# Converted weights split into two whole rows, in a masked-attention and squared-Relu kernel on one core

## The chip, the cores and the metric

The kernel runs on one core of one Trainium2 chip. The time is the device time of one launch in microseconds (us). The engines are TensorE (PE), VectorE (DVE), ScalarE (ACT), GpSimd (POOL) and SyncE (SP), which here issues nearly all DMAs. A weight load of PE is an instruction of its own and runs beside matmuls; the profile calls it PEld.

## What is computed

Causal attention over a window of 128 keys, with a bias that falls linearly with distance, and then two matrix products with a squared Relu between them, all in float32:

```python
# q, k, v: (8, 8, 576, 64); w_in: (512, 2048); w_out: (2048, 512)
scores = (q @ k.T) / sqrt(64) - slope[h] * abs(i - j)     # where 0 <= i - j < 128, else -1e9
attn = softmax(scores)
x = (attn @ v) as (4608 tokens, 512)
h = maximum(x @ w_in, 0)
out = (h * h) @ w_out
```

## The kernel before

The 4608 tokens are cut into 9 chunks of 512 (c), the heads into 4 pairs (p), the 2048 inner columns into 16 blocks of 128 (f). Everything is kept transposed, with the 512 tokens of a chunk along the free axis.

Every float32 operand of a product is split into a high part that PE's fp32r takes exactly and a low part that holds the rest; three products (high x high, high x low, low x high) are summed. `gemm1(c, f)` (L170) makes 12 matmuls of 128 x 128 by 128 x 512 at L178 into the bank `g`, then Relu (L187, ACT), square (L190 on ACT in chunk 0, L193 on DVE later), the high part `hh` (L195, ACT) and the low part `hl` (L197, DVE). `gemm2(c, f)` (L199) makes 12 more at L208 into the four banks `acc`. After block 15 the four banks are copied to output tiles `o` (L220) and sent out (L221). Each matmul comes with its own weight load.

The weights come in as 64-bit floats in pairs of 32-bit words. `weights_load(f)` (L147) brings both matrices' block f as 8 KB a partition into slot f of an arena of 16 slots. `convert(f)` (L154) is five steps in place: two word shifts and a combination, then the high part `wh` (L164, ACT) over the high words and the low part `wl` (L166, DVE) over the low words. So high and low parts lie word by word next to each other, and a matmul's weights are every second word. Until the weights arrive, slots 11 to 15 of the arena serve as room for other things (score tiles `tw`, the bias table `wide`, zeros, the q, k and v of one pair).

The chunks run one after the other. `start` (L593) covers chunk 0: it builds a plan, a list of steps with engine, estimated time, predecessors and a due time, and issues them in the order in which a small list scheduler would run them; among steps that are ready at about the same time on an engine, the one with the earlier due time goes first. In it are: `heat` (L110), 16 pairs of matmuls on zeros of several kinds that fill PE at the beginning; the attention of chunk 0 in 8 segments (steps s, u, e, r, n, z, o, m, x, h, l); the attention of couples 4 to 8 (chunk 1 and the first pair of chunk 2; S scores, V values, `RING` their due times); the 16 conversions (`CONV` their due times, `HOLD` what they wait for); and the products of chunk 0, `gemm2` running two blocks behind.

After that (L706 on) the order on PE is the program's: `gemm1` of step n, `gemm2` of step n - 2, and in every eighth half step a visit, which finishes the values of one couple (`back`, matmuls at L329), loads q, k and v of the one after next, and scores the next (`front`, matmuls at L381, then soft-max on DVE, ACT and POOL). `FIRST` says at which half step the first visit stands. `turn` sends a 128 x 512 tile through DRAM to transpose it (L308 write, L313 read, both issued by SP) and masks the two copies on POOL (L317).

Of the kernel before, what the change touches and what calls it, by code (L numbers as in the profile page):

```python
# [9 lines left out]
F32 = mybir.dt.float32  # L10
F32R = mybir.dt.float32r
BF16 = mybir.dt.bfloat16
I32 = mybir.dt.int32
# [6 lines left out]
B, H, S, D = 8, 8, 576, 64  # L20
NP = H // 2
DM, DF = 512, 2048
NF = DF // 128
# [5 lines left out]
HOLD = lambda f: (('n', 3),) if f < 1 else (('n', 6),) if f < 2 else (('z', 7),)  # L29
# [1 line left out]
HAND = {"SP": 2.0, "PE": 0.25}  # L31
PORT = ('t', 'c', 'h1')
CONVERT = (('Activation', 1.2), ('DVE', 0.7), ('DVE', 1.2), ('Activation', 1.15), ('DVE', 1.2))
RING = lambda q: 50 + 20 * (q - 4)
CONV = lambda f: 28 + 5.5 * f
SOON = (("z", 7),)
FIRST = 35
SYNC = mybir.DependencyInfo(mybir.DependencyClass.Sync, mybir.DependencyReason.DATA)
CST = 256 + 128 * H
ENGINES = {e: getattr(mybir.EngineType, e) for e in ("PE", "DVE", "Activation", "Pool", "SP")}  # L40
# [6 lines left out]
class Kern:  # L47
    def __init__(self, ctx, tc, qkd, vd, w1d, w2d, cstd, outd):
        self.tc, self.nc = tc, tc.nc
        self.qkd, self.vd = qkd, vd  # L50
        self.w1d, self.w2d, self.cstd, self.outd = w1d, w2d, cstd, outd
        ep = lambda name, bufs, **kw: ctx.enter_context(tc.tile_pool(name=name, bufs=bufs, **kw))
        self.c = ep("const", 1)
        self.ld = ep("ld", 3)
        self.tp = ep("tp", 3)
        self.pp = ep("pp", 2)
        self.sm = ep("sm", 6)
        self.xu = ep("xu", 8)
        self.hp = ep("hp", 3)
        self.op = ep("op", 4)  # L60
        self.dr = ep("dr", 4, space=bass.MemoryType.DRAM)
        self.sc = ep("sc", 1, space=PSUM)
        self.at = ep("at", 1, space=PSUM)
        self.g1 = ep("g1", 1, space=PSUM)
        self.ac = ep("ac", 4, space=PSUM)
        self.cst = self.c.tile([128, CST], F32, name="cst")
        self.ident = self.cst[:, 0:128]
        self.mask = self.cst[:, 128:192].bitcast(I32)
        self.never = self.cst[:, 192:256]
        self.raw, self.w = [None] * NF, [None] * NF  # L70
        self.nc.alloc_sbuf_tensor("arena", [128, NF * 2048], F32)
        self.arena = self.nc.sbuf_base - NF * 8192
        self.x, self.qk, self.v, self.h, self.pairs = {}, {}, {}, {}, {}
        at = lambda slot, name, shape: self.nc.alloc_sbuf_tensor_at(name, shape, F32, offset=self.arena + slot * 4096).ap()
        self.wide = [at(2 * (NF - 3), "wide", [128, H, 256])[:, 2 * p : 2 * p + 2] for p in range(NP)]
        self.room_t = [at(2 * (NF - 5) + n, f"tw{n}", [128, 4, 256]) for n in range(4)]
        self.start_banks = [self.ac.tile([128, 512], F32, name="acc") for _ in range(4)]

    def nrel(self, h):
# [16 lines left out]


    def zeros(self):
        at = self.arena + (NF - 2) * 8192
        self.zb = self.nc.alloc_sbuf_tensor_at("zero", [128, 512], BF16, offset=at).ap()  # L100
        self.nc.vector.memset(self.zb, 0.0)
        zr = self.nc.alloc_sbuf_tensor_at("zeros", [128, 1024], F32R, offset=at + 1024).ap()
        self.nc.vector.memset(zr.bitcast(F32), 0.0)
        near = zr[:, 0:512]
        self.kinds = (
            (zr[:, 0:256:2], near), (zr[:, 0:128], near), (zr[:, 0:128], zr[:, 0:1024:2]), (zr[:, 0:64], near),
            (self.zb[:, 0:128], self.zb), (zr[:, 512:640], near),
        )

    def heat(self, n):  # L110
        g = self.g1.tile([128, 512], F32, name="g")
        w, x = self.kinds[4 if n < 4 else n % 6]
        for i in range(2):
            self.nc.tensor.matmul(g[0 : w.shape[1]], w, x, start=i == 0, stop=i == 1)  # L114

    def room(self, c, p, name, shape, offset):
        if (c, p) != (0, NP - 1):
            return self.ld.tile(shape, F32, name=name)  # L120
        at = self.arena + (NF - 1) * 8192 + offset
        return self.nc.alloc_sbuf_tensor_at(f"{name}_", shape, F32, offset=at).ap()

    def load_qk(self, c, p, sg):
# [21 lines left out]

    def weights_load(self, f):  # L147
        nc = self.nc
        at = lambda name, dt: nc.alloc_sbuf_tensor_at(f"{name}{f}", [128, 2, 512, 2], dt, offset=self.arena + f * 8192).ap()
        self.raw[f], self.w[f] = at("raw", I32), at("w", F32R)  # L150
        for i, d in enumerate((self.w1d, self.w2d.rearrange("(f p) d -> f p d", p=128))):
            nc.sync.dma_start(self.raw[f][:, i].rearrange("p d t -> p (d t)"), d[f].bitcast(I32))

    def convert(self, f):  # L154
        nc = self.nc
        lo, hi = self.raw[f][..., 0], self.raw[f][..., 1]
        flo, fhi, wl, wh = lo.bitcast(F32), hi.bitcast(F32), self.w[f][..., 0], self.w[f][..., 1]
        nc.scalar.activation(fhi, fhi, AF.Prelu, scale=2.0**-112, alpha=2.0**32)
        yield
        nc.vector.tensor_scalar(lo, lo, 29, None, op0=ALU.logical_shift_right)  # L160
        yield
        nc.vector.scalar_tensor_tensor(lo, hi, 3, lo, op0=ALU.logical_shift_left, op1=ALU.bitwise_or)
        yield
        nc.scalar.copy(wh, flo)  # L164
        yield
        nc.vector.tensor_tensor(wl, flo, wh.bitcast(F32), op=ALU.subtract)  # L166
# [3 lines left out]
    def gemm1(self, c, f):  # L170
        nc = self.nc
        xs = [self.x[c, p] for p in range(NP)]
        g = self.g1.tile([128, 512], F32, name="g")
        wh, wl = self.w[f][:, 0, :, 1], self.w[f][:, 0, :, 0]
        i = 0
        for cc in range(NCC):
            for w, part in ((wh, 0), (wh, 1), (wl, 0)):
                nc.tensor.matmul(  # L178
                    g, w[:, cc * 128 : cc * 128 + 128], xs[cc][:, part], start=i == 0, stop=i == 11
                )  # L180
                i += 1
        yield
        r = self.hp.tile([128, 512], F32, name="r", bufs=1)
        hh = self.hp.tile([128, 512], F32R, name="hh")
        hl = self.hp.tile([128, 512], F32R, name="hl")
        self.h[c, f] = hh, hl
        nc.scalar.activation(r, g, AF.Relu)  # L187
        if c == 0:
            yield
            nc.scalar.activation(r, r, AF.Square)  # L190
        else:
            yield
            nc.vector.tensor_tensor(r, r, r, op=ALU.mult)  # L193
        yield
        nc.scalar.copy(hh, r)  # L195
        yield
        nc.vector.tensor_tensor(hl, r, hh.bitcast(F32), op=ALU.subtract)  # L197

    def gemm2(self, c, f):  # L199
        nc = self.nc  # L200
        hh, hl = self.h.pop((c, f))
        if f == 0:
            self.acc = self.start_banks if c == 0 else [self.ac.tile([128, 512], F32, name="acc") for _ in range(4)]
        wh, wl = self.w[f][:, 1, :, 1], self.w[f][:, 1, :, 0]
        for m in range(4):
            ms = slice(m * 128, m * 128 + 128)
            for i, (w, h) in enumerate(((wh, hh), (wh, hl), (wl, hh))):
# [1 line left out]
                    self.acc[m], w[:, ms], h, start=(f == 0 and i == 0), stop=(f == NF - 1 and i == 2)  # L209
                )  # L210
            if f == NF - 1:
                o = self.op.tile([128, 512], F32, name="o")
                out = self.outd[m * 128 : m * 128 + 128, 512 * c : 512 * c + 512]
                if c == NCH - 1 and m == 3:
                    nc.scalar.copy(o[:, 0:256], self.acc[m][:, 0:256])
# [377 lines left out]
def start(K):  # L593
    P = Plan()
    for name, n in (("sc", 1), ("sa", 1), ("xa", 1), ("at", 1), ("zp", 1), ("tw", 4), ("t", 3), ("pp", 2), ("ld", 3), ("g", 1)):
        P.room(name, n)
    do = lambda fn, *a: lambda: fn(*a)
# [22 lines left out]

    P.add("zeros", "DVE", 0.4, (), -1, K.zeros)
    for n in range(HEAT):
        P.add(("heat", n), "PE", 0.9 if n < 4 else 0.45, ("zeros",) + ((("heat", n - 1),) if n else ()), 900 + n, do(K.heat, n), "g", "g")

    for k in range(8):
        G = Wide(K, k)
        c, p, sg = G.c, G.p, G.sg
        n = lambda s, *m: (s, k, *m)
# [6 lines left out]
            P.add(n("e", m), "Activation", 0.48 * w, (n("u", m),) + ((n("e", m - 1),) if m else ()), d + 0.5, do(G.exp, m))  # L635
        P.add(n("r"), "DVE", 0.4, (n("e", 3),), d + 1, G.sums)
        P.add(n("n"), "Pool", 2.05 * w, (n("r"),), d + 1, G.norm)
        P.add(n("z"), "PE", 0.9 * w, (n("n"),) + chain("z"), d - 1, G.turn, ("at", "zp", "pp"), "tw")
        P.add(n("o"), "Activation", 0.6, (n("z"),), d + 1, G.out, None, "at")
        P.add(n("m"), "DVE", 0.62 if w == 1 else 0.36, (n("z"),), d + 1, G.also, None, "zp")  # L640
        P.add(n("x"), "PE", 1.0, (n("m"), n("o"), ("v", c, p)) + chain("x"), d + 2, G.values, "xa", "pp")
        P.add(n("h"), "Activation", 0.4, (n("x"),), d + 2, G.high)
        P.add(n("l"), "DVE", 0.36, (n("h"),), d + 2, G.low, None, "xa")
        if sg == 1:
# [1 line left out]
    for q in range(4, 9):  # L646
# [7 lines left out]
        for s in (1, 0):  # L654
# [11 lines left out]
                continue  # L666
            step = do(next, G.squares(), None)
            P.add(n("square"), "DVE", 0.72, (n("n"),), d + 1, step, "pp", "t")
            P.add(n("write"), "SP", 1.6, (n("square"),), d + 1, step)
            P.add(n("read"), "SP", 2.2, (n("write"),), d + 1, step)  # L670
            P.add(n("before"), "Pool", 0.81, (n("read"),), d + 1, step)
            P.add(n("same"), "Pool", 0.81, (n("before"),), d + 1, step)
# [2 lines left out]
    for f in range(NF):  # L675
        d, last = CONV(f), ("w", f)
        g = K.convert(f)
        for i, (engine, us) in enumerate(CONVERT):
            P.add(("c", f, i), engine, us, (last,) + HOLD(f), d, lambda g=g: next(g, None))
            last = ("c", f, i)  # L680

    last = ["wide"] + [("l", k) for k in range(8)]
# [92 lines left out]
```

## Time and profile before

| | |
|---|---|
| time, median of 3 runs (lowest to highest) | 966.18 us (965.46 to 967.34) |
| the profiled execution, time / span | 967.88 us / 966.1 us |
| PE busy | 954.2 us, 99% of the span |
| DVE, ACT, POOL busy | 50%, 43%, 21% |
| granted PE clock, share of full | 0.999 |

The span is from the first to the last instruction; the profiled execution's own time holds some 2 us more. An engine's busy time counts its instructions and not its waiting. Matmuls overlap in the pipeline, so a group's busy time is less than its count times the mean of one. In the chain of waits each piece ends where the next begins, so there the length of 12 matmuls divided by 12 is the step from one to the next.

### The profile page before, as it was taken

To read this page: it belongs to the slowest core of one execution; us is meant where nothing else is said; L and a number is where in the kernel's file an instruction comes from. 1 tells how busy PE (TensorE), PEld (TensorE's weight loads), DVE (VectorE), ACT (ScalarE), POOL (GpSimd) and SP (SyncE) were. 2 spreads that over 40 slices of the span, in tenths; PEclk is the share of its full clock that TensorE was granted. 3 is DMA by queue.
4 is the path that set the end of the run, shared out by engine and by line. 5 is a ranking of instruction groups with operands and counts; after the bars stand their busy time and mean duration, and the time that the engine had idled before them with its cause. 6 is when DMAs were issued, how large, how long until landed. Compare 5 with 4: busy or idle time off the path is not lost.

```text
span 966.1 us, 17340 instructions
## 1 busy us (share of the span) xinstructions
PE 954.2 (99%) x6392; PEld 792.3 (82%) x6392; DVE 486.2 (50%) x1330; ACT 418.0 (43%) x1112; POOL 201.1 (21%) x252
## 2 busy tenths in 40 slices
PE   9899999999999999999999999999999999999998
PEld 5688887888888888888888888888888888888886
DVE  6898865444554444454545454444444454423222
ACT  7899754334433434334444444333433344322221
POOL 4122232222122222222121222122222222100000
PEclk9999999999999999999999999999999999999999
DMA  9983434222432223333422232233322231101001
GB/s 350 405 296 113 131 77 149 71 76 73 126 82 83 73 66 113 82 83 82 126 74 80 80 107 77 77 83 99 98 70 69 82 101 45 44 1 44 1 1 44
DMA packets 73028, 95.11 MB, mean 98 GB/s; under 512 B 8048, under 2 KB 42224, under 8 KB 72944
## 3 DMA queue, kind: packets, MB, share of 16 engines
q1 hardware_dynamic: 72512, 93.49, 32.0%
q8 instruction: 50, 0.82, 0.4%
q10 hardware_dynamic: 432, 0.52, 0.2%
q14 instruction: 34, 0.28, 0.1%
HBM read 67.76 MB, written 26.21 MB: 97 GB/s over the span
## 4 chain that ended last, share of the span: by engine, by line
PE 95%; DMA 2%; DVE 1%; ACT 1%; POOL 1%; issue 0%; SPq 0%; POOLq 0%; ACTq 0%
PE acc L208 41%; PE g L178 40%; PE at L329 6%; PE s L381 2%; PE g L381 2%; PE g L114 1%; DMA way<-pp 1%; DMA pp<-way 1%; PE acc L282 1%; PE s L496 0%; SPq L308 0%; PE at L528 0%; PE acc L496 0%; POOL pp L317 0%; PE at L381 0%
## 5 line engine op out<-in xcount | busy, mean ns | idle before, releaser
L178 PE MATMUL g<-xu,w 128*128 128x512 f32 x1728 | 426.9, 396 | 1.6 <-ACT r L187 1.6
L178 PEld LDWEIGHTS g<-xu,w 128*128 128x128 f32 x1728 | 337.2, 196 | 67.3 <-ACT r L187 3.4
L208 PE MATMUL acc<-hh,w 128*128 128x512 f32 x1152 | 388.0, 398 | 0.0
L208 PEld LDWEIGHTS acc<-hh,w 128*128 128x128 f32 x1152 | 225.3, 196 | 44.7 <-issue 0.5
L193 DVE TENSOR_TENSOR r<-r 128x512 f32<-128x512 f32 x128 | 92.5, 723 | 272.3 <-ACT r L187 272.2
L208 PE MATMUL acc<-hl,w 128*128 128x512 f32 x576 | 227.6, 395 | 0.0
L187 ACT ACTIVATE r<-g 128x512 f32<-128x512 f32 x144 | 85.5, 594 | 319.9 <-PE g L178 310.6
L317 POOL TENSOR_SCALAR_AFFINE_SELECT pp<-pp 128x512 f32<-128x512 f32 x128 | 103.7, 811 | 238.2 <-DMA way<-pp 129.7
L197 DVE TENSOR_TENSOR hl<-r,hh 128x512 fp32r<-128x512 f32 x144 | 107.8, 749 | 75.9 <-ACT hh L195 74.7
L195 ACT CAST hh<-r 128x512 fp32r<-128x512 f32 x144 | 89.2, 620 | 116.1 <-DVE r L193 115.5
L208 PEld LDWEIGHTS acc<-hl,w 128*128 128x128 f32 x576 | 112.8, 196 | 20.2
L253 POOL TENSOR_TENSOR t<-t,nm 128x512 f32<-128x512 f32 x64 | 73.3, 1147 | 252.7 <-DVE nm L250 220.5
L242 ACT ACTIVATE t<-t,nm 128x128 f32<-128x128 f32 x256 | 99.4, 390 | 37.1 <-DVE nm L235 37.1
L329 PEld LDWEIGHTS at<-pp,v 128*64 128x64 f32 x1024 | 55.2, 137 | 14.9 <-issue 10.4
L329 PE MATMUL at<-pp,v 128*64 128x128 f32 x1024 | 63.6, 276 | 2.7 <-POOL pp L317 2.6
L427 DVE COPY_PREDICATED t<-cst,s 64x256 f32<-64x256 int32 x100 | 44.3, 443 | 32.2 <-ACT t L415 18.5
L235 DVE CUSTOM_DVE_ANT_0 t<-t,cst 128x128 f32<-128x128 f32 x256 | 59.0, 294 | 0.9
L304 DVE STREAM_TRANSPOSE pp<-t 128x512 f32<-128x512 f32 x64 | 45.3, 708 | 23.9 <-POOL t L253 21.1
L242 ACT ACTIVATION_READ_ACCUMULATOR t<-t,nm 128x1 f32 x256 | 47.9, 187 | 0.0
L381 PE MATMUL s<-qk 64*64 64x64 f32 (+2 forms) x1168 | 47.5, 252 | 0.0
L381 PEld LDWEIGHTS s<-qk 64*64 64x64 f32 x1168 | 43.0, 134 | 0.0
L417 POOL MEMSET t<- 64x128 f32 (+1 forms) x44 | 10.0, 228 | 137.7 <-PE g L381 130.9
(65 smaller groups left out, 475.4 us busy)
## 6 DMA issues: line engine op xcount, KB each, us to landing
raw<-in_dram SPq DMA_DIRECT2D x32, 512.0 KB, 8.7
way<-pp SPq DMA_DIRECT2D x256, 64.0 KB, 1.8
pp<-way SPq DMA_DIRECT2D x64, 256.0 KB, 2.7
qk<-in_dram SPq DMA_DIRECT2D x32, 320.0 KB, 3.6
v<-in_dram SPq DMA_DIRECT2D x32, 320.0 KB, 2.9
qk<-in_dram SPq DMA_DIRECT2D x38, 256.0 KB, 4.2
out_dram<-o SPq DMA_DIRECT2D x35, 256.0 KB, 2.8
v<-in_dram SPq DMA_DIRECT2D x3, 256.0 KB, 4.6
```

The source lines that it names most:

```text
L178: nc.tensor.matmul(g, w[:, cc * 128 : cc * 128 + 128], xs[cc][:, part], start=i == 0, stop=i == 11)
L187: nc.scalar.activation(r, g, AF.Relu)
L193: nc.vector.tensor_tensor(r, r, r, op=ALU.mult)
L195: nc.scalar.copy(hh, r)
L197: nc.vector.tensor_tensor(hl, r, hh.bitcast(F32), op=ALU.subtract)
L208: nc.tensor.matmul(self.acc[m], w[:, ms], h, start=(f == 0 and i == 0), stop=(f == NF - 1 and i == 2))
L235: self.nc.vector.tensor_tensor_reduce(self.t[:, m], self.t[:, m], self.K.nrel(2 * self.p + m // 2), -0.125, BIG, ALU.add, ALU.min, self.nm ...
L242: self.nc.scalar.activation(self.t[:, m], self.t[:, m], AF.Exp, bias=nm[:, m : m + 1], scale=-1.0, accum_out=nm[:, 4 + m : 5 + m],)
L253: self.nc.gpsimd.tensor_tensor(self.t, self.t, self.nm[:, 8:12].unsqueeze(2).to_broadcast([128, 4, 128]), op=ALU.mult)
L317: nc.gpsimd.affine_select(to, self.own, pattern=[[-32 * sign, 4], [0, 4], [-sign, 32]], compare_op=op, fill=0.0, base=0, channel_multiplie ...
L329: self.nc.tensor.matmul(self.X[r, o : o + 128].rearrange("p (a c) -> p a c", a=4), v[:, 2 * sg + k, r], src[:, :, 2 * j + i], start=sg == ...
L381: mm = nc.tensor.matmul(to, qk[r, q0 : q0 + 64], qk[r, k0 : k0 + 64 * n], start=True, stop=True, skip_group_check=True,)
```

## The change

The arena gets a seventeenth slot. Raw words of block f go to slot f + 1, the converted weights of block f to slot f, as [low or high][matrix][512], so each part is one row of 512 words per matrix. The write of `wh` of block f overwrites raw words of block f - 1, so a predecessor is added: the last step of the conversion of block f - 1. The rooms that share the arena move up one slot. The pool of four output tiles goes, and four quarters of the spare slot take its place. The heats are all bf16. Visits come two half steps (one product pair) later. Some due times and one predecessor change, and with them the order in which steps are issued.

```diff
-RING = lambda q: 50 + 20 * (q - 4)
-CONV = lambda f: 28 + 5.5 * f
-SOON = (("z", 7),)
-FIRST = 35
+RING = lambda q: 50 + 18 * (q - 4)
+CONV = lambda f: 34 + 5.5 * f
+SOON = (("x", 7),)
+FIRST = 37
@@ Kern.__init__
-        self.op = ep("op", 4)
...
-        self.nc.alloc_sbuf_tensor("arena", [128, NF * 2048], F32)
+        self.nc.alloc_sbuf_tensor("arena", [128, (NF + 1) * 2048], F32)
...
+        o = at(2 * NF, "o", [128, 4, 512])
+        self.o = [o[:, m] for m in range(4)]
@@ heat
-        w, x = self.kinds[4 if n < 4 else n % 6]
         for i in range(2):
-            self.nc.tensor.matmul(g[0 : w.shape[1]], w, x, start=i == 0, stop=i == 1)
+            self.nc.tensor.matmul(g, self.zb[:, 0:128], self.zb, start=i == 0, stop=i == 1)
@@ weights_load
-        at = lambda name, dt: nc.alloc_sbuf_tensor_at(f"{name}{f}", [128, 2, 512, 2], dt, offset=self.arena + f * 8192).ap()
-        self.raw[f], self.w[f] = at("raw", I32), at("w", F32R)
+        at = lambda slot, name, shape, dt: nc.alloc_sbuf_tensor_at(f"{name}{f}", shape, dt, offset=self.arena + slot * 8192).ap()
+        self.raw[f] = at(f + 1, "raw", [128, 2, 512, 2], I32)
+        self.w[f] = at(f, "w", [128, 2, 2, 512], F32R)
@@ convert
-        flo, fhi, wl, wh = lo.bitcast(F32), hi.bitcast(F32), self.w[f][..., 0], self.w[f][..., 1]
+        flo, fhi, wl, wh = lo.bitcast(F32), hi.bitcast(F32), self.w[f][:, 0], self.w[f][:, 1]
@@ gemm1
-        wh, wl = self.w[f][:, 0, :, 1], self.w[f][:, 0, :, 0]
+        wh, wl = self.w[f][:, 1, 0], self.w[f][:, 0, 0]
@@ gemm2
-        wh, wl = self.w[f][:, 1, :, 1], self.w[f][:, 1, :, 0]
+        wh, wl = self.w[f][:, 1, 1], self.w[f][:, 0, 1]
...
-                o = self.op.tile([128, 512], F32, name="o")
+                o = self.o[m]
@@ start
-        P.add(n("z"), "PE", 0.9 * w, (n("n"),) + chain("z"), d - 1, G.turn, ("at", "zp", "pp"), "tw")
+        P.add(n("z"), "PE", 0.9 * w, (n("n"),) + chain("z"), d - 5.5, G.turn, ("at", "zp", "pp"), "tw")
...
-        P.add(n("x"), "PE", 1.0, (n("m"), n("o"), ("v", c, p)) + chain("x"), d + 2, G.values, "xa", "pp")
+        P.add(n("x"), "PE", 1.0, (n("m"), n("o"), ("v", c, p)) + chain("x"), d + 4, G.values, "xa", "pp")
...
-            P.add(n("write"), "SP", 1.6, (n("square"),), d + 1, step)
+            P.add(n("write"), "SP", 1.6, (n("square"),), d - 4, step)
...
-            P.add(("c", f, i), engine, us, (last,) + HOLD(f), d, lambda g=g: next(g, None))
+            free = (("c", f - 1, len(CONVERT) - 1),) if f and i == 3 else ()
+            P.add(("c", f, i), engine, us, (last,) + HOLD(f) + free, d, lambda g=g: next(g, None))
```

## Rows read from the trace of the kernel before

**Rows 1.** The page: busy time of PE, and the chain's shares by line.

```profile
PE 954.2 (99%) x6392; PEld 792.3 (82%) x6392; DVE 486.2 (50%) x1330; ACT 418.0 (43%) x1112; POOL 201.1 (21%) x252
...
PE acc L208 41%; PE g L178 40%; PE at L329 6%; PE s L381 2%; PE g L381 2%; PE g L114 1%; DMA way<-pp 1%; DMA pp<-way 1%; PE acc L282 1%; PE s L496 0%; SPq L308 0%; PE at L528 0%; PE acc L496 0%; POOL pp L317 0%; PE at L381 0%
```

**Rows 2.** The chain in order of time: start, length (us), what.

```profile
53.11 2.80 PE g L178 x12
...
214.68 2.76 PE g L178 x12
```

**Rows 3.** Groups by line and form: busy us, mean ns | idle before.

```profile
L178 PE MATMUL g<-xu,w 128*128 128x512 f32 x1728 | 426.9, 396 | 1.6 <-ACT r L187 1.6
...
L178 PEld LDWEIGHTS g<-xu,w 128*128 128x128 f32 x1728 | 337.2, 196 | 67.3 <-ACT r L187 3.4 <-issue 0.3
```

**Rows 4.** Timeline of PE where it waits: start, length (us), what [wait].

```profile
42.82 3.10 PE L178 MATMUL g<-xu,w 128*128 128x512 f32 x12 [1.59 <-ACT r L187]
...
137.46 2.33 PE L329 MATMUL at<-pp,v 128*64 128x128 f32 x32 [0.59 <-POOL pp L317]
...
150.95 0.66 PE L329 MATMUL at<-pp,v 128*64 128x128 f32 x8 [1.53 <-POOL pp L317]
152.06 0.66 PE L329 MATMUL at<-pp,v 128*64 128x128 f32 x8 [0.46 <-POOL pp L317]
```

**Rows 5.** The chain near 151 us.

```profile
150.97 1.05 POOL pp L317
```

**Rows 6.** Line 114, weights with step 1: ns min/median/max, first and last start.

```profile
L114 PEld LDWEIGHTS g<-zeros x2: 187/188/189, 8.8 to 9.0; 128*128 128x128 f32 x2
L114 PE MATMUL g<-zeros x2: 388/442/497, 8.8 to 9.2; 128*128 128x512 f32 x2
...
L114 PE MATMUL g<-zeros x2: 397/440/482, 25.7 to 26.0; 128*128 128x512 f32 x2
```

**Rows 7.** Line 114, weights with step 2.

```profile
L114 PEld LDWEIGHTS g<-zeros x2: 195/197/199, 9.6 to 9.7; 128*128 128x128 f32 x2
L114 PE MATMUL g<-zeros x2: 397/452/506, 9.6 to 10.0; 128*128 128x512 f32 x2
```

**Rows 8.** Line 114, 64 weight columns and bf16; last the bf16 pair in the timeline.

```profile
L114 PEld LDWEIGHTS g<-zeros x2: 137/138/138, 22.7 to 22.8; 128*64 128x64 f32 x2
L114 PE MATMUL g<-zeros x2: 388/433/478, 22.7 to 23.0; 128*64 128x512 f32 x2
...
L114 PE MATMUL g<-zero x2: 376/376/377, 23.5 to 23.7; 128*128 128x512 bf16 x2
...
23.48 0.59 PE L114 MATMUL g<-zero 128*128 128x512 bf16 x2
```

**Rows 9.** Line 114, moving operand with step 2, at 29.5 us.

```profile
L114 PE MATMUL g<-zeros x2: 651/684/717, 29.5 to 30.1; 128*128 128x512 f32 x2
```

**Rows 10.** Groups by line: subtractions of 512 (whole rows) and 1024 elements (every second word).

```profile
L197 DVE TENSOR_TENSOR hl<-r,hh 128x512 fp32r<-128x512 f32 x144 | 107.8, 749 | 75.9 <-ACT hh L195 74.7 <-PE acc L208 0.7
...
L166 DVE TENSOR_TENSOR w<-raw,w 128x1024 fp32r<-128x1024 f32 x16 | 19.4, 1220 | 0.8 <-ACT w L164 0.7
```

**Rows 11.** The chain: the second pair with a strided moving operand.

```profile
29.52 1.19 PE g L114 x2
```

**Rows 12.** Busy us (instructions) of PE, PEld, DVE, ACT, POOL; PEclk, DMA share, GB/s.

```profile
50.00:75.00 25.00, 25.00 (x132) 20.92 (x131) 22.46 (x56) 22.90 (x46) 5.74 (x8) 1.00 0.80 288
```

**Rows 13.** Timeline of DVE: last steps of conversions 6 and 7, 8 and 9.

```profile
66.24 2.36 DVE L166 TENSOR_TENSOR w<-raw,w 128x1024 fp32r<-128x1024 f32 x2
...
81.16 2.32 DVE L166 TENSOR_TENSOR w<-raw,w 128x1024 fp32r<-128x1024 f32 x2
```

**Rows 14.** Timeline of PE: the first products of blocks 6 and 8.

```profile
69.75 2.96 PE L178 MATMUL g<-xu,w 128*128 128x512 f32 x12
...
84.55 2.92 PE L178 MATMUL g<-xu,w 128*128 128x512 f32 x12
```

**Rows 15.** The page, DMA issues: the output tiles, KB each, us to landing.

```profile
out_dram<-o SPq DMA_DIRECT2D x35, 256.0 KB, 2.8
```

More of the change, by code (lines that the diff above doesn't have):

```diff
@@ L70, in __init__ @@
         self.raw, self.w = [None] * NF, [None] * NF
-        self.nc.alloc_sbuf_tensor("arena", [128, NF * 2048], F32)
-        self.arena = self.nc.sbuf_base - NF * 8192
+        self.nc.alloc_sbuf_tensor("arena", [128, (NF + 1) * 2048], F32)
+        self.arena = self.nc.sbuf_base - (NF + 1) * 8192
         self.x, self.qk, self.v, self.h, self.pairs = {}, {}, {}, {}, {}
         at = lambda slot, name, shape: self.nc.alloc_sbuf_tensor_at(name, shape, F32, offset=self.arena + slot * 4096).ap()
-        self.wide = [at(2 * (NF - 3), "wide", [128, H, 256])[:, 2 * p : 2 * p + 2] for p in range(NP)]
-        self.room_t = [at(2 * (NF - 5) + n, f"tw{n}", [128, 4, 256]) for n in range(4)]
+        self.wide = [at(2 * (NF - 2), "wide", [128, H, 256])[:, 2 * p : 2 * p + 2] for p in range(NP)]
+        self.room_t = [at(2 * (NF - 4) + n, f"tw{n}", [128, 4, 256]) for n in range(4)]
+        o = at(2 * NF, "o", [128, 4, 512])
+        self.o = [o[:, m] for m in range(4)]
         self.start_banks = [self.ac.tile([128, 512], F32, name="acc") for _ in range(4)]
@@ L98, in zeros, with heat @@
     def zeros(self):
-        at = self.arena + (NF - 2) * 8192
+        at = self.arena + (NF - 1) * 8192
         self.zb = self.nc.alloc_sbuf_tensor_at("zero", [128, 512], BF16, offset=at).ap()
         self.nc.vector.memset(self.zb, 0.0)
[L102 to L110, printed above, removed]
+    def heat(self):
         g = self.g1.tile([128, 512], F32, name="g")
-        w, x = self.kinds[4 if n < 4 else n % 6]
         for i in range(2):
-            self.nc.tensor.matmul(g[0 : w.shape[1]], w, x, start=i == 0, stop=i == 1)
+            self.nc.tensor.matmul(g, self.zb[:, 0:128], self.zb, start=i == 0, stop=i == 1)
     def room(self, c, p, name, shape, offset):
@@ L120, in room @@
             return self.ld.tile(shape, F32, name=name)
-        at = self.arena + (NF - 1) * 8192 + offset
+        at = self.arena + NF * 8192 + offset
         return self.nc.alloc_sbuf_tensor_at(f"{name}_", shape, F32, offset=at).ap()
@@ L622, in start @@
     for n in range(HEAT):
-        P.add(("heat", n), "PE", 0.9 if n < 4 else 0.45, ("zeros",) + ((("heat", n - 1),) if n else ()), 900 + n, do(K.heat, n), "g", "g")
+        P.add(("heat", n), "PE", 0.9 if n < 4 else 0.45, ("zeros",) + ((("heat", n - 1),) if n else ()), 900 + n, K.heat, "g", "g")
     for k in range(8):
```

## The prediction

> **What bounds the kernel now.** I read the page first, then the groups by line, the chain of waits, the timeline of the stretches where TensorE (PE) is not fed, and the warm-up matmuls of line 114 one pair at a time. PE is busy 954.2 us of the 966.1 us span, and nothing else comes near; the chain that ended last is four fifths L208 and L178, the two matrix products [rows 1]. So two things can move the time: the step from one product matmul to the next, and the few places where PE stands still.
>
> The step: 9 chunks x 16 blocks x 24 matmuls are 3456, in 288 groups of 12. In the chain a group takes 2.80 us, or 2.76 us in some stretches [rows 2]: 233.3 or 230 ns a matmul. Of the 195 longest pieces listed, 191 are such groups, nearly all of 2.80 us or slightly more where a stretch begins, so some 97 groups are of the shorter kind; the mean step is (191 x 233.3 + 97 x 230) / 288 = 232.2 ns, 802 us in all. The reader is to see that a weight load of 196 ns goes with every matmul and that PE hardly ever waits between them [rows 3].
>
> The stops: the matmuls of V7 wait 0.59 us for a GpSimd (POOL) selection; the first visit's (the values of couple 8) wait 1.53 and 0.46 us for the same; the second block's product waits 1.59 us for the Relu of the first [rows 4, 5]. The sum is made against the profiled run, 967.88 us with a span of 966.1; it was 1.7 us above the median of 966.18, and the change of time is carried over to the median.
>
> **The weights in one piece.** Loads read 128 words that lie side by side, no longer every second one. The trace has that experiment: heat's kinds load with step 2, with step 1, 64 columns only, and in bf16. Step 1 loads in 187 to 189 ns, step 2 in 195 to 199 [rows 6, 7]: some 8 ns less per load. The load is not what paces, though. In each pair the second matmul has no load beside it. Its duration less 162 ns is the step it allows: bf16 has 376 ns, and two of them take 0.59 us, a step of 0.214 us [rows 8]; the products' 396 ns go with 233 [rows 3]. Step 1 shows 388 ns at 8.8 us and 397 at 25.6 us, step 2 shows 397 [rows 6, 7], 64 columns show 388, with a load 50 ns shorter still [rows 8]. So an fp32 matmul is slow by itself, load or no load, and the same layout gives both 388 and 397. The bounds are 388 everywhere (step 226: 3456 x 6.2 = 21 us less) and 397 everywhere (step 235: 3456 x 2.8 = 10 us more). I take 0, because the late pair, in the same stretch of the run as the products, is at 397 with step 1. The step switching between 230 and 233.3 from stretch to stretch with one layout says that this term can drift: all at 230 would be 3456 x 2.2 = 7.6 us less, all at 233.3 3.8 us more.
>
> [...]
>
> The conversions do the same work: the DVE subtraction of 1024 elements took 1220 ns into every second word, and the 512-element one into a whole row 749 [rows 10], so per element the plain output is no cheaper. Term: 0, bounds +-0.1 us per block, beside other work.
>
> **The moved visits (FIRST 35 to 37).** A visit now comes one product pair later, 2 x 2.8 = 5.6 us of PE work. It takes with it its loads, eight writes and two reads on SP's queue, the selections and scalings on POOL, and the copies on ACT and DVE; the four output DMAs of a chunk are then ahead of it on SP instead of behind. In steady state all of that is far from the bound. The gain is in the first visit: the values of couple 8 waited until POOL's selection ended at 152.02 us [rows 5], for 1.53 + 0.46 us on PE. Started 5.6 us later they find their data 2 us old. Bounds 0 to -2.3 us; I take -2.0. What is late next is PE itself. The last visit ends hundreds of microseconds of products before the end, so nothing is added there.
>
> **The issue list.** Couples 4 to 8 get earlier due times (18 us apart, not 20), their DRAM writes too, and conversions get due times 6 us later. Only steps that are ready together change places. V7's wait of 0.59 us should shrink (0 to -1.0 with the half that follows it, I take -0.6). The second product's 1.59 us behind ACT's copies for couple 4 [rows 4] can go either way by the same amount; I take 0. All sixteen heats are now bf16: the strided-moving one at 29.52 us held the chain for 1.19 us [rows 11] where a bf16 pair takes 0.59 [rows 8]; I take -0.5, between 0 and -2 for all of them together.
>
> The added wait: wh of block f (ACT) now waits for wl of block f-1 (DVE), which reads the raw words it overwrites. Queued behind it on ACT are Relu, Square and hh of chunk 0, and PE waits for those through g. ACT and DVE are 90% busy at 50 to 75 us [rows 12], so the cover is thin: wl of block 6 ends at 66.24 + 1.2 = 67.4 us, its product starts at 69.75; of block 8 at 82.3, started at 84.55 [rows 13, 14]. About 2.2 us of cover in both. I take 0 lost; without the cover every microsecond of lateness is one of time, up to 6.
>
> The output tiles in the spare slot are four as before, each rewritten a chunk of 16 x 5.6 us after it was sent; I take 0. They are now quarters of one tensor, though. If a copy into one waited for the DMA out of the one before, which takes 2.8 us to land [rows 15], three waits of 2.8 us would meet a cover of one product, 2.8 us [rows 2], and a visit's matmuls (32 of L329 took 2.33 us with a wait in them [rows 4]; with the scores, an estimate of 3.3 us): 2.3 us for each of 8 chunks, 18 us at the other end (E below).
>
> Sum: 0 - 2.0 - 0.6 + 0 - 0.5 + 0 = -3.1 us; 966.2 - 3.1 = **963.1 us**. With the drift left at its present mix, this case has 961 to 966.
>
> **Rivals.**
> A, the step falls: contiguous loads end 8 ns earlier and every matmul starts that much sooner or settles in the quicker state. For it: 388 ns in the first step-1 pair. Against: 397 in the later one, and 388 with 64 columns whose load is 50 ns shorter, so the duration does not follow the load. All at 230 gives 955 us, all at 226 gives 942.
> B, the whole excess over bf16's step is the layout: 3456 x (232.2 - 214) = 63 us less, 900 us. Against it: step-1 pairs at 388 and 397, not 376. [...]
> C, slower: conversions come late. With later due times and the chain wh(f) after wl(f-1), block 6 or 8 misses its product. It decides when a conversion is later than 2.2 us; the due shift of 6 us at worst costs 6 - 2.2 = 3.8 us on one block, and twice that if a later block, already without cover, slips again by the same. Less the 3.1 gained: 967 to 971 us.
> D, the change doesn't do what it says: the reordered list puts couple 8's selections as much later as the visit moved, the old waits return elsewhere, about 966 us.
> E, the output copies wait for one another's DMAs, 963.1 + 18 = 981 us; against it, nothing in the kernel's order asks for it.
>
> **How the numbers follow.** Forecast case 0.48 (0.30 of it faster, 0.16 same, 0.02 slower), A 0.22 (0.21 faster, 0.01 same), B 0.02, C 0.15 (0.04 same, 0.11 slower), D 0.10 (0.08 same, the rest split), E 0.03. Faster by over 0.2% is below 964.2, slower above 968.1, about what a measurement of this kernel can tell from no change. Faster 0.54, same 0.29, slower 0.17. For 8 in 10 the range leaves out B and E, the lower half of A and the upper part of C: 946 to 968.5.
>
> **What would show it.** Right: groups of 12 still at 2.76 to 2.80 us, weight loads at 188 instead of 196 ns, no PE wait before L329 near 150 us. A right: the same groups at 2.71 to 2.76. C: idle time of PE before L178 released by DVE's w, between 60 and 130 us. What would make the prediction wrong is a step that follows the load's length, or an issue list that starves PE before 40 us, where I have priced nothing but the heats.

## The result, and the profile after

The changed kernel takes 968.69 us (968.23 to 969.86), the kernel before, run beside it, 966.33: a ratio of 1.0024, with an interval of 1.0013 to 1.0034. I had forecast 963.1, in a range of 946 to 968.5. The profiled execution took 968.72 us, its span is 967.0.

The page after, busy time of PE and the chain by line, and one issue row (KB each, us to landing):

```profile
PE 956.9 (99%) x6389; PEld 767.2 (79%) x6392; DVE 481.5 (50%) x1329; ACT 419.1 (43%) x1112; POOL 204.9 (21%) x252
...
PE acc L202 42%; PE g L172 42%; PE at L323 6%; PE s L375 2%; PE g L375 2%; PE g L107 1%; PE acc L276 1%; PE at L522 0%; PE s L490 0%; PE acc L490 0%; PE at L375 0%; PE acc L525 0%; DVE w L160 0%; DVE raw L154 0%; DVE t L421 0%
...
out_dram<-o SPq DMA_DIRECT2D x35, 256.0 KB, 2.1
```

The groups by line (busy us, mean ns | idle before), the answer to [rows 3]. Lines stand some six lower: L178 is now L172, L208 L202, L329 L323, L166 L160, L114 L107.

```profile
L172 PE MATMUL g<-xu,w 128*128 128x512 f32 x1728 | 428.9, 397 | 0.7 <-ACT r L181 0.7
...
L172 PEld LDWEIGHTS g<-xu,w 128*128 128x128 f32 x1728 | 324.7, 188 | 80.8 <-ACT r L181 1.1
```

All waits of PE after (us in total, times, longest):

```profile
PE acc L276 <- DVE xu L289: 2.2, 1, 2.2
PE g L107 <- DVE zero L102: 1.3, 1, 1.3
PE s L375 <- DVE t L425: 0.8, 1, 0.8
PE g L172 <- ACT r L181: 0.7, 1, 0.7
PE g L107 <- issue: 0.2, 1, 0.2
```

And the chain in the middle of the kernel (start, us, what), the answer to [rows 2]:

```profile
503.32 2.81 PE g L172 x12
506.14 2.81 PE acc L202 x12
508.95 2.81 PE g L172 x12
```

The reader is to see three things. The loads got shorter as forecast, 188 for 196 ns. The waits for POOL's selections near 137 and 151 us [rows 4] are gone. And a group of 12 products, which took 2.80 or 2.76 us before [rows 2], takes 2.81 or 2.82 in the chain wherever it does not open a stretch. From the starts of the matmuls, without the first of each stretch (a stretch is a row of products with nothing else on PE between them), the mean step is 234.25 ns after, and 232.92 in the profiled execution before. In nearly every stretch seven matmuls take 1640 ns, 234.29 each.

The starts of some products (us) show where the time went. "Words" is the changed kernel with the old word-by-word weights, "moving 64" the fastest kernel found; both are below.

| product | before | after | words | moving 64 |
|---|---|---|---|---|
| first, chunk 0 block 0 | 38.13 | 37.67 | 37.71 | 36.51 |
| chunk 1, block 4 | 168.25 | 165.31 | 165.04 | 163.31 |
| chunk 5, block 0 | 556.20 | 555.14 | 552.86 | 547.84 |
| last of `gemm2` | 961.27 | 962.10 | 957.11 | 950.14 |
| end | 966.09 | 966.96 | 961.91 | 954.98 |

By 168 us the change is 2.9 us ahead, as the sum of 3.1 had it. From there on it loses 3.8 us at an even pace, some 1.3 ns on each of the 3000 products that are left.

### The profile page after: what moved, and what is told of

Read it like the earlier page. It is cut to its first block, busy times and chain, and to the rows that moved or that the text cites. A ratio compares the mean times of both kernels' runs of the same rounds, so it can differ in the third digit from the quotient of the medians.

```text
span 967.0 us, 17325 instructions
## 1 busy us (share of the span) xinstructions
PE 956.9 (99%) x6389; PEld 767.2 (79%) x6392; DVE 481.5 (50%) x1329; ACT 419.1 (43%) x1112; POOL 204.9 (21%) x252
## 4 chain that ended last, share of the span: by engine, by line
PE 98%; DVE 1%; issue 0%; ACT 0%; DVEq 0%
PE acc L202 42%; PE g L172 42%; PE at L323 6%; PE s L375 2%; PE g L375 2%; PE g L107 1%; PE acc L276 1%; PE at L522 0%; PE s L490 0%; PE acc L490 0%; PE at L375 0%; PE acc L525 0%; DVE w L160 0%; DVE raw L154 0%; DVE t L421 0%
## 5 line engine op out<-in xcount | busy, mean ns | idle before, releaser
L172 PE MATMUL g<-xu,w 128*128 128x512 f32 x1728 | 428.9, 397 | 0.7 <-ACT r L181 0.7
L202 PE MATMUL acc<-hh,w 128*128 128x512 f32 x1152 | 389.6, 399 | 0.0
L172 PEld LDWEIGHTS g<-xu,w 128*128 128x128 f32 x1728 | 324.7, 188 | 80.8 <-ACT r L181 1.1
L202 PEld LDWEIGHTS acc<-hh,w 128*128 128x128 f32 x1152 | 216.9, 188 | 54.3 <-issue 0.3
L202 PE MATMUL acc<-hl,w 128*128 128x512 f32 x576 | 228.2, 396 | 0.0
L311 POOL TENSOR_SCALAR_AFFINE_SELECT pp<-pp 128x512 f32<-128x512 f32 x128 | 106.6, 834 | 236.4 <-DMA way<-pp 130.9
L191 DVE TENSOR_TENSOR hl<-r,hh 128x512 fp32r<-128x512 f32 x144 | 104.5, 726 | 71.0 <-ACT hh L189 70.3
L202 PEld LDWEIGHTS acc<-hl,w 128*128 128x128 f32 x576 | 108.6, 188 | 25.1
L323 PEld LDWEIGHTS at<-pp,v 128*64 128x64 f32 x1024 | 55.2, 137 | 11.7 <-issue 11.7
L323 PE MATMUL at<-pp,v 128*64 128x128 f32 x1024 | 63.0, 276 | 0.0
```

Source lines behind the costliest of these rows:

```text
L172: nc.tensor.matmul(g, w[:, cc * 128 : cc * 128 + 128], xs[cc][:, part], start=i == 0, stop=i == 11)
L202: nc.tensor.matmul(self.acc[m], w[:, ms], h, start=(f == 0 and i == 0), stop=(f == NF - 1 and i == 2))
L311: nc.gpsimd.affine_select(to, self.own, pattern=[[-32 * sign, 4], [0, 4], [-sign, 32]], compare_op=op, fill=0.0, base=0, channel_multiplie ...
L323: self.nc.tensor.matmul(self.X[r, o : o + 128].rearrange("p (a c) -> p a c", a=4), v[:, 2 * sg + k, r], src[:, :, 2 * j + i], start=sg == ...
```

## The experiments

**1. The layout alone.** Theory: the longer step comes of the weights' new layout, and everything else is worth about -3. Rival: the loss comes of another part (order, output tiles). The changed kernel with high and low words side by side again:

```diff
-        self.w[f] = at(f, "w", [128, 2, 2, 512], F32R)
+        self.w[f] = at(f, "w", [128, 2, 512, 2], F32R)
...
```

> The changed kernel with the weights again word by word (high and low interleaved), everything else as changed. Theory L (the layout sets the step): steps of 230 and 233.3 ns in stretches return, 3456 x 1.3 ns = 4.6 us less than the changed kernel's 968.7, so 964.1 us, below both kernels. Theory O (the new order and the moved visits set the phase in which a stretch starts, and so its step): the step stays at 234.3 ns and the time at 968.7 us.

964.14 us, 0.9969 (0.9957 to 0.9981). The waits of PE are those of the changed kernel; the loads are back at 195 ns, and most groups at 2.80. A group of the changed kernel in the chain:

```profile
900.65 2.81 PE g L172 x12
```

Two groups of the kernel with words, at about the same time:

```profile
901.51 2.80 PE g L172 x12
904.31 2.80 PE acc L202 x12
```

Its mean step is 232.65 ns. So all else together is worth what was forecast, and rows in place of words cost (1.0024 - 0.9969) x 966 = 5.3 us; by the steps, 3456 x 1.6 ns = 5.5 us.

**2. The step by itself.** Behind the last product of the changed kernel stand sets of 49 matmuls that differ in where their weights and their moving operand begin and how far apart the words of the weights lie; three sets have fewer columns:

```diff
+        for ww, xx in plan:
+            g = self.g1.tile([128, 512], F32, name="g")
+            for _ in range(49):
+                self.nc.tensor.matmul(g[0 : ww.shape[1], 0 : xx.shape[1]], ww, xx, start=True, stop=True)
```

> The changed kernel with 11 x 49 extra matmuls on its own weights and x at the end (their results are not used): weights with step 1, 2, 4 and 8 words, step 1 and 2 from the next word on, step 3, 64 columns, 256 and 384 moving columns, a moving operand that starts one word later. Theory L: step 1 gives 234.3 ns, step 2 gives 230 or 233.3; if the reading of weights and of the moving operand get into each other's way, steps 4 and 8 differ again. Theory M (the moving operand alone sets the step): all the 512-column sets agree, 64 weight columns too, and 256 and 384 columns take the same share of it per column. Time 968.7 + about 120 us.

> The changed kernel with 30 sets of 49 extra matmuls at the end (results not used): weights with step 1 from words 0, 1, 2, 3, 4, 8, 16, 64; step 2 from words 0, 2, 4, 16; moving operands that start 1 to 64 words later; step-2 and step-1 sets behind 1 to 6 small matmuls of 64 columns. Theory P (how a stretch starts sets its step): step 2 gives 230 behind some numbers of small matmuls and 233.3 behind others, step 1 gives 234.3 and 233.3 in the same way. Theory A (the address sets it): the step follows the word from which weights or moving operand start and not the small matmuls.

The timeline of PE (start, length in us). In the first run: weights with step 1, step 2, step 8; step 1 beginning one word later; step 1 with the moving operand one word later.

```profile
961.79 11.64 PE L176 MATMUL g<-xu,w 128*128 128x512 f32 x49
973.49 11.56 PE L176 MATMUL g<-xu,w 128*128 128x512 f32 x49
...
997.09 12.31 PE L176 MATMUL g<-xu,w 128*128 128x512 f32 x49
1009.46 11.70 PE L176 MATMUL g<-xu,w 128*128 128x512 f32 x49
...
1047.81 11.88 PE L176 MATMUL g<-xu,w 128*128 128x512 f32 x49
```

In the second: step 1 beginning 3 words and 64 words later.

```profile
1010.03 11.55 PE L180 MATMUL g<-xu,w 128*128 128x512 f32 x49
...
1056.87 11.74 PE L180 MATMUL g<-xu,w 128*128 128x512 f32 x49
```

Less some 0.40 us for the last matmul, each is 48 steps. In every set but the first of a run the first step is longer, by some 0.1 us (0.23 with step 4 and 8), so the lengths alone would give too much: 232.5 ns for step 2. From the starts of the matmuls behind the first step: 234.3 ns with step 1, 230.0 with step 2, 235.5 with step 4, 243.3 with step 8, and for step 1 that begins later by 1, 2, 3, 4, 8, 16 and 64 words 233.3, 233.3, 230.2, 233.2, 232.4, 233.3 and 234.3. With step 1 and the moving operand one word on it is 237.3, with step 2 and the moving operand 1, 2, 4, 8 words on 235.4, 233.4, 231.9, 230.0. Step 1 from word 0 gave 234.2 to 234.3 in each of its five sets. With 64 weight columns it is 231.4, with 256 moving columns 118.6, with 384 173.3. So the product's step is not the load's length: step 2 loads longer (194 ns for 188) and steps shorter. Nor is it the clock: the granted clock was 1.00 and 0.999 in the two runs. Where the two operands begin decides, so theory M is out, and 64 words, 256 bytes, bring the same value back.

> The changed kernel with 40 sets of 49 extra matmuls at the end (results not used): eight layouts (weights step 1 from words 3 and 7; step 2 with the moving operand 64 and 8 words on; step 2 from words 4, 16 and 1; step 1 from word 3 with the moving operand 8 words on), each behind 1 to 5 small matmuls. Theory P (the start of a stretch decides): a layout that gave 230 once gives 233.3 behind other starts too. Theory A (the address decides): it gives 230 behind every start.

Eight layouts, five times each, behind one to five small matmuls. Step 1 from word 3, step 2 from word 4, and step 2 with the moving operand 8 words on settled at 230.0 each time. Step 2 from word 1, and step 2 with the moving operand 64 words on, gave 230.0 or 233.3 as the start would have it; step 1 from word 7 gave 231.7 or 233.3, and step 2 from word 16 gave 233.4, once 235.5. Step 1 from word 3 with the moving operand 8 words on gave 233.3 to 233.4 each time, where the same weights with the moving operand in place gave 230.0 (start, length):

```profile
962.30 11.52 PE L177 MATMUL g<-xu,w 128*128 128x512 f32 x49
...
1044.96 11.68 PE L177 MATMUL g<-xu,w 128*128 128x512 f32 x49
```

So the address of the weights alone does not decide; the places of both do. Some layouts had one step behind all five starts, and others settle in one of two, which is the mixture that [rows 2] showed for the kernel before.

**3. The moving operand moved.** The kernel before with bf16 heats and FIRST 37 (the last kernel of section 6), and the x and h tiles 32 bytes on, at multiples of 64:

```diff
-        warm = self.c.tile([128, 1], F32, name="warm")
+        warm = self.c.tile([128, 16], F32, name="warm")[:, 0:1]
```

> The same kernel with weights where they were and all tiles of x and h 32 bytes further on, so that the moving operands start at multiples of 64 bytes. Step 2 from word 0 with the moving operand 8 words on gave 230 ns behind all five starts. Theory A: 230 ns in all stretches, 0.985. Theory P: 0.995.

956.83 us, 0.9895 (0.988 to 0.991), the fastest of all: 10 us below the kernel before. The chain shows 2.76 in most stretches, 2.80 still in some, so I had expected too much (230 ns in all stretches, 0.985): five starts in the sets were too few to call this layout's step fixed.

```profile
400.01 2.76 PE g L178 x12
402.77 2.76 PE acc L208 x12
```

The mean step is 230.85 ns, 1.9 less than without the shift (232.77): 3456 x 1.9 = 6.6 us, and by the spans 961.4 - 955.0 = 6.4 (by the ratios, 0.9949 - 0.9895, 5.2). The same line in the changed kernel:

> The kernel after with the x and h tiles 32 bytes further on, so that a moving operand starts at a multiple of 64 bytes; nothing else changes. If the step hangs on how weights and moving operand lie to one another, the 234.28 ns of the kernel after is no property of weights in one piece, and another value appears: 230.0 to 233.4 ns, which on 3456 products is 0.9 ns to 4.3 ns each, so 954 to 966 us. If the layout of the weights alone decides, the step stays at 234.28 ns and the time at 968 to 970 us. The waits should stand as in the kernel after either way.

965.57 us, 0.9987 (0.9977 to 0.9996). The chain:

```profile
501.97 2.80 PE g L172 x12
504.77 2.80 PE acc L202 x12
```

233.33 ns in nearly all stretches in place of 234.29, with the same weights and, within 0.3 us, the same waits. So 234.29 is a property of the pair of addresses, not of weights in one piece.

**4. The weights moved.** In the kernel with bf16 heats and FIRST 37, weights 16 bytes on; in the changed kernel, weights 12 bytes, raw words and output tiles 32 bytes on, in slots of the old length. In both the arena is 64 bytes longer, and x and h, which lie behind it, move 64 bytes with it:

```diff
-        self.nc.alloc_sbuf_tensor("arena", [128, (NF + 1) * 2048], F32)
+        self.nc.alloc_sbuf_tensor("arena", [128, (NF + 1) * 2048 + 16], F32)
...
-        self.raw[f] = at(f + 1, "raw", [128, 2, 512, 2], I32)
-        self.w[f] = at(f, "w", [128, 2, 2, 512], F32R)
+        self.raw[f] = at(f + 1, "raw", [128, 2056], I32)[:, 8:2056].rearrange("p (a d t) -> p a d t", a=2, t=2)
+        self.w[f] = at(f, "w", [128, 2051], F32R)[:, 3:2051].rearrange("p (a b d) -> p a b d", a=2, b=2)
```

> The kernel of heats and first visit (interleaved weights) with its weights 16 bytes further on. Step 2 from word 4 gave 230 ns behind all five starts, from word 0 behind one of six. Theory A: 230 ns in all stretches, 3456 x 2.8 = 9.6 us less, a ratio of 0.985 in place of 0.9949. Theory P: the mixture of 230 and 233.3 stays, 0.995.

> The changed kernel with its converted weights 3 words (12 bytes) further on in memory, and raw words and output tiles 32 bytes further on; nothing else. Step-1 weights from word 3 gave 230 ns behind all five starts, from word 0 234.3 behind all. Theory A (the address of the weights decides): step 230, 3456 x 4.3 = 14.8 us less than the changed kernel, 954 us, a ratio of 0.987. Theory P (the alternating operands of the real stream hide it): 233.3 or more, a ratio of 0.999 to 1.002.

996.55 us (1.0305) and 993.8 us (1.0286). The step fell: 231.1 ns in the first, and 230.0 to 230.2 in nearly all stretches of the second. That the second met 230.0 is luck, though. I took the value from a set with the moving operand in place, and here the moving operand had moved 64 bytes too, a pair of places that no set had.

```profile
501.90 2.76 PE g L172 x12
504.66 2.76 PE acc L202 x12
```

The start was lost: the product of chunk 1, block 4 began 36 us late in the first (200.23 against 163.89 without the shift) and 34 us late in the second (199.44 against 165.31). From there to the end the second kernel needs 789.3 us, where the changed kernel needs 801.7. Waits of PE, and the last step of the conversions, in the second:

```profile
PE g L172 <- ACT w L158: 12.6, 4, 3.6
PE at L323 <- POOL pp L311: 5.8, 1, 5.8
PE g L172 <- DVE w L160: 5.3, 2, 4.9
```

```profile
L160 DVE TENSOR_TENSOR w<-raw,w 128x1024 fp32r<-128x1024 f32 x16 | 20.4, 1272 | 21.4 <-PE g L172 16.4 <-ACT w L158 4.6
```

The conversion is no slower to the shifted place (1272 ns, 1334 in the changed kernel). It waits 16.4 us for products, in five waits, each for the last matmul of `gemm1` of the block before. My theory: a piece now reaches 12 bytes into the next slot, and the write there is held until the product that reads the neighbour is done. Idle time is not all that was lost: up to that mark PE is idle 31.8 us, 26.5 more than in the changed kernel up to its own. Part of the other 8 us goes with the clock (busy us of PE, PEld, DVE, ACT, POOL; PEclk, DMA share, GB/s):

```profile
25.00:50.00 25.00, 16.89 (x153) 12.74 (x152) 16.98 (x41) 14.78 (x27) 3.91 (x5) 0.80 0.77 278
...
75.00:100.00 25.00, 16.34 (x126) 12.84 (x125) 15.41 (x38) 12.94 (x29) 5.85 (x8) 0.81 0.76 262
```

In these stretches, where PE was busy 16.9 and 16.3 of 25 us, the granted clock was 0.80 and 0.81 of full, and 0.93 between them. From 45 to 101 us 24 steps between products took some 427 ns, together 4.6 us more than at 234; in the changed kernel the clock was 1.00 throughout, and no step without a wait was over 344 ns. To test the theory, slots 32 bytes longer:

> The kernel after with the weights of blocks 0 to 13 starting 12 bytes after a multiple of 64, as in the run with weights 12 bytes on, but with slots 32 bytes longer, so that no piece of one block reaches into the slot of the next; blocks 14 and 15 stay as they are (no room). If the early loss of that run (some 31 us by the first product of block 4 of the second stripe) came of the order that overlapping slots force, and not of where the bytes lie, it is gone here: the marks up to that product stand within 2 us of the kernel after, 14 blocks of 16 step at 230.0 ns, two at 234.3 ns, and 967 us falls by 3456 x 14/16 x 4.2 ns = 12.7 us, to 954 to 957 us. If conversions or loads are slower to such addresses themselves, the loss comes back and the time is 980 us or more.

964.76 us, 0.9976 (0.9965 to 0.9986). The early loss is gone, the products of chunk 1 stand within 0.9 us of the changed kernel's, and the same line has

```profile
L162 DVE TENSOR_TENSOR w<-raw,w 128x1024 fp32r<-128x1024 f32 x16 | 20.8, 1301 | 0.1
```

So the overlap cost the 34 us, not the 12 bytes as such. My 230.0 ns for 14 blocks was wrong, though, and through a slip that shows more than the run meant to: with slots 32 bytes longer every block begins at another place, and its products have another step. The arena is 448 bytes longer here, and x and h moved with it. Worked out from the starts of `gemm1` in chunks 3 to 7 without the first step of each, in ns (blocks 14 and 15 without the 12 bytes):

```
block  0     1     2     3     4     5     6     7     8     9     10    11    12    13    14    15
step   235.3 235.3 231.5 233.1 230.9 233.3 230.0 233.3 235.0 235.4 231.4 233.1 230.9 233.3 234.6 234.7
```

Blocks 0 to 5 and 8 to 13 agree within 0.3 ns, at a distance of 8 x 32 = 256 bytes. In the changed kernel, with slots of 8192 bytes, all 16 blocks lie between 234.1 and 234.5. Count the distance from the start of the moving operand to that of the weights, modulo 256 bytes (96 in the changed kernel, as the kernels allocate them): block 6, at 108, has 230.0, as step 1 from word 3 had; block 5, at 76, has 233.3, as word 3 with the moving operand 8 words on had; blocks 14 and 15, at 96, have the step that they have in the changed kernel, 234.3, within 0.4 ns. Block 4, at 44, has 230.9, where the run with 12 bytes, at the same distance, has 230.0 to 230.2. So the distance fits better than either address alone, but no run was made to test that.

**5. The order.** Here the question was which part of the edit brought the 3 us. Four kernels: the changed kernel with the due times and FIRST of the kernel before; the changed kernel with FIRST 35 alone; the other way, the kernel before with all new due times and FIRST 37; and the changed kernel with words and the old due times of z and x. The edit of the first, in part:

```diff
-RING = lambda q: 50 + 18 * (q - 4)
-CONV = lambda f: 34 + 5.5 * f
-SOON = (("x", 7),)
-FIRST = 37
+RING = lambda q: 50 + 20 * (q - 4)
+CONV = lambda f: 28 + 5.5 * f
+SOON = (("z", 7),)
+FIRST = 35
...
-        P.add(n("z"), "PE", 0.9 * w, (n("n"),) + chain("z"), d - 5.5, G.turn, ("at", "zp", "pp"), "tw")
+        P.add(n("z"), "PE", 0.9 * w, (n("n"),) + chain("z"), d - 1, G.turn, ("at", "zp", "pp"), "tw")
...
```

> The changed kernel with before's due times and first visit at half step 35: layout, output tiles, heats and the added predecessor stay as changed. Theory L: step 234.3 ns and before's waits of 2 to 3 us, so 966.3 + 4.6 = 970.9 us. Theory O: steps as before, about 966.3 us.

975.54 us, 1.0088 (1.0074 to 1.0102): 4.6 us above what I had expected with theory L. The step is 234.3, as there, but the waits are longer. PE in the timeline, where it waits:

```profile
140.42 3.38 PE L323 MATMUL at<-pp,v 128*64 128x128 f32 x32 [4.08 <-POOL pp L311]
...
154.64 0.66 PE L323 MATMUL at<-pp,v 128*64 128x128 f32 x8 [1.20 <-POOL pp L311]
155.79 0.66 PE L323 MATMUL at<-pp,v 128*64 128x128 f32 x8 [0.49 <-POOL pp L311]
```

> The changed kernel with the first visit at half step 35 again, due times as changed. If the moved visit is what removed the wait on POOL's selections, 2.0 us of it return: 970.7 us. If the earlier due times of couple 8 alone removed it: 968.7 us.

969.4 us, 1.0020 (1.0012 to 1.0029), and no wait at L323 comes back. With the new due times the later visit is worth nothing.

> The kernel before with the changed due times and the first visit at half step 37, nothing else: weights word by word, old slots, old heats, no added predecessor. If the issue list by itself carries the 3 us that the changed kernel gains in its waits: 963 to 964 us, as with the interleaved weights in the changed kernel (964.1). If the list only fits the added predecessor and the bf16 heats: 966 us or more.

968.51 us, 1.0004 (0.9995 to 1.0013). The waits at the values are gone, but the first product starts at 39.20 us, 1.07 later than before, and conversions are late, once each:

```profile
PE g L178 <- DVE w L166: 1.0, 1, 1.0
...
PE g L178 <- ACT w L164: 0.4, 1, 0.4
```

So the list by itself brings nothing; it fits the other edits.

> The changed kernel with interleaved weights and with before's due times for the z and x steps of chunk 0. With the order alone changed the first product came 1.07 us later than before. If the due times of z and x do that: first product at 36.6 us instead of 37.7, 1.1 us less than with interleaved weights alone, a ratio of 0.9957. If the later conversions do it: no change, 0.9969.

965.22 us, 0.9972 (0.9961 to 0.9982), against 0.9969 with words: no gain. The first product comes at 37.45 us for 37.71, and two late conversions at 58 to 60 us (1.4 us together) take it back.

**6. Predecessor, heats, visit.** Each alone in the kernel before; the last has bf16 heats and FIRST 37:

```diff
+            free = (("c", f - 1, len(CONVERT) - 1),) if f and i == 3 else ()
-            P.add(("c", f, i), engine, us, (last,) + HOLD(f), d, lambda g=g: next(g, None))
+            P.add(("c", f, i), engine, us, (last,) + HOLD(f) + free, d, lambda g=g: next(g, None))
```

```diff
-        w, x = self.kinds[4 if n < 4 else n % 6]
+        w, x = self.kinds[4]
```

> The kernel before with the added predecessor alone (wh of a block after wl of the block before it). The changed kernel with the old due times waited 4.1 us for POOL before V7 where the kernel before waits 0.6. If the predecessor makes that wait: some 4 us more than before, 970 to 971 us. If the slots or the heats make it: as before, 966 to 967 us.

971.77 us, 1.0040 (1.0027 to 1.0054). No product waits for a conversion; the values of V7 wait for POOL:

```profile
141.61 3.62 PE L329 MATMUL at<-pp,v 128*64 128x128 f32 x32 [4.54 <-POOL pp L317]
...
155.86 1.34 PE L329 MATMUL at<-pp,v 128*64 128x128 f32 x14 [0.97 <-POOL pp L317]
```

The selections before V7 end at 142.35 us, 4.15 later than before (138.20), though the last conversion starts only 0.5 later (126.5 for 126.0).

> The kernel before with all 16 heats in bf16, nothing else. Forecast priced this at -0.5 us, between 0 and -2: the first product starts earlier than 38.13 us by that much. Rival: the heats only fill waits, and the first product starts when it did, within 0.2 us.

965.51 us, 0.9979 (0.9970 to 0.9988): 2.0 us. The first product starts 1.52 us earlier than before, and the second still waits:

```profile
36.61 3.09 PE L178 MATMUL g<-xu,w 128*128 128x512 f32 x12
41.31 3.07 PE L178 MATMUL g<-xu,w 128*128 128x512 f32 x12 [1.61 <-ACT r L187]
```

> The kernel before with bf16 heats and the first visit at half step 37, nothing else. The first visit's wait on POOL (2.3 us with bf16 heats alone) should be gone: that kernel's ratio of 0.9979 less 2.3 us, some 0.9955, about 963.2 us against 967.6 for the kernel before. Rival: POOL's selections come later with the visit, and the wait returns: 0.998.

962.88 us, 0.9949 (0.9937 to 0.9962), by the ratios 2.9 us less than with the heats alone. In the old order the later visit does what I forecast for it; of the waits at L329, 2.8 us with the heats alone, this is left:

```profile
PE at L329 <- POOL pp L317: 0.4, 1, 0.4
```

## Why the prediction was wrong, point by point

**Weights in one piece, 0 forecast, 4.6 us measured.** This is the step that failed, and it turned a gain into a loss. I had its bounds (-21 to +10 us) and the right reading that the load does not pace: 188 ns against 196 went with a longer step. But I took 0 on the late pair of heats, at 397 ns with step 1 [rows 6]. By my own rule, the duration less 162, that pair said 235 ns; I called it the same as the products, which showed 396 [rows 3], though 1 ns on 3456 matmuls is 3.5 us. A pair of two matmuls also can't show a pattern that repeats after seven, and it read other addresses than the products do. I had counted 232.2 ns for the step before; the matmul starts give 232.9. In the changed kernel it is 234.25: 3456 x 1.33 = 4.6 us. Of these 3.8 us fall behind the product of chunk 1, block 4; the rest is already in the 2.9 us gained by then, and -2.9 + 3.8 is the +0.9 of the spans. The medians differ by 2.4 us: the profiled execution of before lay 1.55 us above its median, and whether that was step or wait, one trace can't show.

**Step kinds.** "This term can drift" was right for words and wrong for rows: the mixture of 230 and 233.3 ns is what the old layout has, and the new one is fixed at 234.29. Rival A, a shorter step, had the wrong cause (the load's end) and a real effect at other addresses: 230.0 ns with weights 12 bytes and the moving operand 64 bytes on, and 956.83 us with the moving operand moved. Rival B is out: no layout tried settled below some 230 ns. So is D: nothing on PE waits for POOL any more.

**The moved visit, -2.0.** Right in the old order (2.9 us with FIRST 37 on top of the heats), nothing in the new one (FIRST 35 gives 1.0020, 37 gives 1.0024). The wait it was to remove had been removed by the list.

**V7's wait, -0.6.** It is gone, but not by itself: the added predecessor alone makes it 4.5 us, and the new due times undo that. Rival C had the right edit and the wrong place: in the changed kernel no product waits for a conversion (the kernel before with the new list alone has 1.4 us of that), but the added predecessor delays the selections on which the values wait. By which steps the delay gets from the conversions to POOL no run separates. With the old due times and FIRST 35 the changed kernel is 6 us slower still. I had put the predecessor at 0 with a bound of 6.

**Heats, -0.5.** They are worth 1.5 us at the first product and 2.0 in the time, the edge of my range. The new list gives 1.07 back there: -1.52 + 1.07 = -0.45, and the mark shows -0.46. That loss shows as the wait of 2.2 us at L276 for `xu` (0.8 us at the same matmuls before, L282), in the stretch before 40 us that I had left unpriced.

**The second product's 1.59 us [rows 4], 0.** It fell to 0.7.

**Output tiles, 0.** Right. No wait of PE or of the copies stands behind them, and the tiles land in 2.1 us, for 2.8 before [rows 15]; E is out.

**The sum** of all but the layout, -3.1, was right as a sum (-3.0 in the kernel with words) with three of its parts wrong. Agreement of a total does not vouch for its terms.

## What to carry to other kernels

Where one instruction repeats thousands of times, price a new layout by the step of a long set of that very instruction at the very addresses, not by a few instances elsewhere: a nanosecond was 3.5 us here, more than any single wait of PE. When operands are given other places in memory, look at where each begins within 256 bytes, as one would look at a buffer's size, and at what else the edit moves: a longer arena moved the moving operands in three of these runs. And undo the parts of a combined edit one at a time: two of them here removed the same wait, and one made the wait that another took away.

## What the runs showed of the hardware

The step between 128 x 512 fp32r matmuls, each with its load, depends on where weights and moving operand begin: 230.0 to 235.4 ns among layouts with 128 words in a row, 237.3 ns with the moving operand one word on. Each time it was tried, 256 bytes of distance brought the same values back (234.3 ns again with weights 64 words on, within 0.3 ns between blocks 0 to 5 and 8 to 13). What lies beneath no run here shows, and I leave it open. I also could not say beforehand which address gives 230.0; it was found by trying.

With one moving operand, the weights' step and start alone moved the matmul's step between 230.0 and 235.5 ns (243.3 with step 8, whose loads take 327 ns, longer than the step itself). So where the weights lie cost these matmuls time, although the loads ran beside them. Whether it is bandwidth that is lost, no run shows.

The same layout can also hold one of two steps, 230.0 or 233.3, for a whole stretch, according to how the stretch began. Step 2 with the moving operand 8 words on is one of these: it gave 230.0 behind all five starts in the sets, and 233.3 in some stretches of the kernel at 956.83 us. By an estimate from these two steps, 3.3 ns on each of 96 products is 0.3 us a stretch, so two executions of one kernel could differ by some microseconds (there is one trace of each kernel, so this is not shown), and it is why single profiles were compared here by their steps and not by their ends.
